# Two loads for x's first tiles and a new order of the opening in a dense Mish block

## The chip, the cores and the metric

The kernel runs on one NeuronCore of a Trainium2 chip. The metric is the device time of one execution in microseconds, as the median of several runs; lower is better. The profile comes from one execution taken by the hardware profiler, whose times are counted from the first instruction.

## The reference

```python
B, S, D, F = 1, 2048, 512, 1792     # all bf16
def reference(x, w1, b1, w2):
    h = jnp.einsum("bsd,df->bsf", x, w1) + b1
    sp = jnp.log1p(jnp.exp(-jnp.abs(h))) + jnp.where(h > 0, h, jnp.zeros_like(h))
    act = h * jnp.tanh(sp)          # Mish
    return jnp.einsum("bsf,fd->bsd", act, w2)
```

Two matrix products with a bias and the Mish activation between them: 2048 rows of 512 become 2048 rows of 1792, and then rows of 512 again.

## The kernel before

TensorE multiplies a stationary 128x128 tile with a moving tile of up to 512 columns, and contracts over the partitions. For the first product, x must therefore lie transposed, as `xT` (512 rows in KT = 4 tiles, named k, by 2048 columns); w1 lies as 4 tiles k by 1792 columns, in FT = 14 tiles named f. The 2048 rows of x are worked in four blocks of 512. For each block and each f, four matmuls (`mm1_step`, L176; one for each k) sum into one PSUM bank, ScalarE reads the bank with Mish and the bias (L159) into `a_sb`, and TensorE then makes the second product, 14 matmuls of 512 columns for each tile of 128 rows (`mm2_step`, L198). VectorE copies the result out of PSUM (L204), and SyncE stores it.

Every engine has a queue of its own which runs in the order in which the program writes it; the class `Stream` keeps for each a counter, and `wait` puts a semaphore wait into the queue. All order is thus written by hand.

The opening is special, since the data is still coming. TensorE runs eight matmuls on constants (`WARM`, L105) which serve no result. The first 256 rows of x are loaded as they lie into `x_nat`, one load for both tiles of 128, and TensorE transposes them by matmuls with an identity (`transpose_x`, L145): eight of 128 columns, in four PSUM banks, copied out into `xT` by VectorE and ScalarE (L150). Rows 256 to 511 and the other blocks come through transposing DMAs on SyncE's queue. Of w1, the first eight f (`OPEN`) are loaded as four pieces by k: k 0 and k 2 are issued by ScalarE, k 1 and k 3 by SyncE, all at L85. The first block's matmuls for these eight f then run k by k over eight PSUM banks, bank (4 + f) mod 8, in the order in which the pieces arrive (`first`): first k 0 for tile 0, and for tile 1, then k 1 and k 2 for both, then tiles 2 and 3 for k 0 to 2, and at the end k 3 for all 512 columns. `spread_b1` turns the bias on VectorE (L246, L248) before the first Mish needs it.

The two tiles of the first load hold even and odd rows of x, so that each partition reads one run of 2 KB; `rows` gives the stores of output tiles 0 and 1 the same order.

Of the kernel before, what the change touches and what calls it, by code (L numbers as in the profile page):

```python
# [4 lines left out]

P = 128
SQ = 32
WARM = (512,) * 5 + (256,) * 2 + (128,)
BLOCKS = (512, 512, 512, 512)


# [21 lines left out]
def bass_standalone__dense_activation_mish__prompt_kernel(  # L33
# [16 lines left out]
    x2, out2 = x[0], out[0]  # L50
# [3 lines left out]
    OPEN = 8  # L54
    N0 = BLOCKS[0] // P

    with ExitStack() as es:
        def sb(name, shape, t):
            return es.enter_context(nc.sbuf_tensor(name, shape, t))

        x_nat = sb("x_nat", [P, 2, D], BF)
        xT = sb("xT", [P, KT, S], BF)
# [5 lines left out]
        diff = sb("diff", [P, P], dt.int32)  # L68
        ident = sb("ident", [P, P], BF)
        a_sb = sb("a_sb", [P, FT, S], BF)  # L70
        o_sb = sb("o_sb", [P, S // P, D], BF)
        ps = es.enter_context(nc.psum_tensor("ps", [P, 8, 512], F32))

        def sem(name):
            return es.enter_context(nc.semaphore(name))

        sp = Stream(nc.sync, None)
        pe = Stream(nc.tensor, sem("c_pe"))
        dve = Stream(nc.vector, sem("c_dve"))
        act = Stream(nc.scalar, sem("c_act"))  # L80
        pool = Stream(nc.gpsimd, sem("c_pool"))

        def load(q, dst, src, name, transpose=False):
            s = sem(name)
            (q.eng.dma_start_transpose if transpose else q.eng.dma_start)(dst, src).then_inc(s, 16)  # L85
            return (s, 16)

        def load_w1(q, ks, a, b):
            return load(q, w1_sb[:, ks, a * P:b * P], w1v[:, ks, a * P:b * P], "s_w1_%d_%d" % (ks.start, a))
# [6 lines left out]
        def load_part(q, k0, k1, a, b):  # L96
            t = load_w1(q, slice(k0, k1), a, b)
            for f in range(a, b):
                for k in range(k0, k1):
                    t_w1[k, f] = t  # L100

        t_bz = dve.mark(nc.vector.memset(b1_nat[:, :], 0.0))  # L102
        c_w = nc.const_aps.tensor(1.0, [P, P], BF)
        c_m = nc.const_aps.tensor(1.0, [P, 512], BF)
        t_fill = [pe.mark(nc.tensor.matmul(ps[:, 7, 0:n], c_w, c_m[:, 0:n], start=True, stop=True)) for n in WARM]  # L105

        act.eng.preload_act_table(ACT.Mish)  # L107
        act.wait(t_bz)
        for k in (0, 2):
            load_part(act, k, k + 1, 0, OPEN)  # L110
        t_xn = load(sp, x_nat[:, :, :], x2[0:2 * P, :].rearrange("(p j) d -> p j d", p=P), "s_xn")
        load_part(sp, 1, 2, 0, OPEN)
        sp.wait(t_fill[2])
        t_x23 = load(sp, xT[:, :, 2 * P:4 * P], x2[2 * P:4 * P, :], "s_x23", True)
        load_part(sp, 3, 4, 0, OPEN)
# [3 lines left out]
        t = load(sp, w2_sb[:, :, :], w2v, "s_w2")  # L119
# [3 lines left out]
        for s in range(1, len(BLOCKS)):  # L123
            lo, hi = starts[s], starts[s + 1]
            t_xT.append(load(sp, xT[:, :, lo:hi], x2[lo:hi, :], "s_xT%d" % s, True))


        t_diff = pool.mark(pool.eng.iota(diff[:, :], pattern=[[1, P]], base=0, channel_multiplier=-1))  # L128
        dve.wait(t_diff)
        t_id = dve.mark(nc.vector.tensor_scalar(ident[:, :], diff[:, :], 0, None, ALU.is_equal))  # L130

        free = [[] for _ in range(8)]
        t_cp = {(j, k): t_x23 for j in (2, 3) for k in range(KT)}
        t_mish = {}

        def transpose_x():

            pe.wait(t_xn, t_id)
            for bank, (eng, js, ks) in enumerate(((dve, (0,), (0,)), (act, (1,), (0,)), (dve, (0, 1), (1,)),
                                                  (act, (0, 1), (2, 3)))):  # L140
                n, m = len(ks), len(js)
                for i, k in enumerate(ks):
                    for h, j in enumerate(js):
                        lo = (i * m + h) * P
                        mm = nc.tensor.matmul(ps[:, bank, lo:lo + P], x_nat[:, j, k * P:(k + 1) * P], ident[:, :],  # L145
                                              start=True, stop=True)
                eng.wait(pe.mark(mm))
                dst = xT[:, ks[0]:ks[0] + n, js[0] * P:(js[-1] + 1) * P]
                src = ps[:, bank, 0:n * m * P].rearrange("p (k t) -> p k t", k=n)
                t = eng.mark(nc.vector.tensor_copy(dst, src) if eng is dve else act.eng.activation(dst, src, ACT.Copy))  # L150
                for k in ks:
                    for j in js:
                        t_cp[j, k] = t
                free[bank] = [t]

        def mish(s, f, bank, t_mm):
            n = BLOCKS[s]
            act.wait(t_b1c, t_mm)
            t = act.mark(act.eng.activation(a_sb[:, f, starts[s]:starts[s + 1]], ps[:, bank, 0:n], ACT.Mish,  # L159
                                            bias=b1_sb[:, f:f + 1]))  # L160
            t_mish[s, f] = t
            free[bank] = [t]

        def mm1_step(s, f, k, bank, js=None):

            n = BLOCKS[s]
            lo, hi = (0, n) if js is None else (js[0] * P, (js[-1] + 1) * P)
            first = k == 0 and lo == 0
            if first:
                pe.wait(*free[bank])  # L170
            pe.wait(t_w1[k, f])
            if s:
                pe.wait(t_xT[s])
            else:
                pe.wait(*[t_cp[j, k] for j in (js or range(N0))])
            return nc.tensor.matmul(ps[:, bank, lo:hi], w1_sb[:, k, f * P:(f + 1) * P],  # L176
                                    xT[:, k, starts[s] + lo:starts[s] + hi], start=first, stop=(k == KT - 1 and hi == n))
# [8 lines left out]

        def rows(i):

            if i < 2:
                return out2[0:2 * P, :].rearrange("(p j) d -> p j d", p=P)[:, i, :]  # L190
            return out2[i * P:(i + 1) * P, :]

        def mm2_step(i, f, lo, hi, bank):
# [7 lines left out]
        def put(i, lo, hi, bank, t_mm, q=sp):  # L201
            nonlocal n_out
            dve.wait(t_mm)
            t = dve.mark(nc.vector.tensor_copy(o_sb[:, i, lo:hi], ps[:, bank, 0:hi - lo]))  # L204
            free[bank] = [t]
            q.wait(t)
            q.eng.dma_start(rows(i)[:, lo:hi], o_sb[:, i, lo:hi]).then_inc(s_out, 16)
            n_out += 1
# [8 lines left out]
        def mm2_last(i):  # L217

            nonlocal n_out
            cuts = (0, D - 3 * P // 2, D - P // 2, D)  # L220
            toks = []
            for n, eng in enumerate((dve, dve, act)):
                lo, hi, bank = cuts[n], cuts[n + 1], (i + n) % 4
                for f in range(FT):
                    mm = mm2_step(i, f, lo, hi, bank)
                eng.wait(pe.mark(mm))
                dst, src = o_sb[:, i, lo:hi], ps[:, bank, 0:hi - lo]
                t = eng.mark(nc.vector.tensor_copy(dst, src) if eng is dve else act.eng.activation(dst, src, ACT.Copy))  # L228
                toks.append((lo, hi, t))
            for q, lo, hi, t in ((sp, 0, toks[1][1], toks[1][2]), (act,) + toks[2]):  # L230
                q.wait(t)
                q.eng.dma_start(rows(i)[:, lo:hi], o_sb[:, i, lo:hi]).then_inc(s_out, 16)
                n_out += 1

        def first(fs, js, ks, last=False):
            for k in ks:
                for f in fs:
                    mm = mm1_step(0, f, k, (4 + f) % 8, js)
                    if last and k == KT - 1:
                        mish(0, f, (4 + f) % 8, pe.mark(mm))  # L240


        def spread_b1():
            dve.wait(t_b1)
            for j in range(P // SQ):
                t = dve.mark(nc.vector.transpose(b1_T[j * SQ:(j + 1) * SQ, :], b1_nat[:, j * SQ:(j + 1) * SQ]))  # L246
            dve.wait(t)
            return dve.mark(nc.vector.tensor_copy(b1_sb[:, :], b1_T[:, 0:FT]))  # L248

        transpose_x()  # L250
        t_b1c = spread_b1()
        first(range(4), (0,), (0,))
        first(range(4), (1,), (0,))
        first(range(4, OPEN), (0, 1), (0,))
        first(range(OPEN), (0, 1), (1, 2))
        first(range(OPEN), (2, 3), (0, 1, 2))
        first(range(OPEN), None, (3,), True)
# [42 lines left out]
```

## Time and profile before

| | |
|---|---|
| median of 3 runs | 104.91 us (104.37, 104.91, 105.55) |
| span of the profiled execution, first to last instruction | 104.0 us |
| TensorE busy | 101.4 us, 98% of the span, 520 matmuls |
| ScalarE busy | 39.5 us, 38% |
| VectorE busy | 13.2 us, 13% |
| bytes moved by DMA | 7.94 MB, mean 76 GB/s |

The profile gives for the profiled execution its span alone; what lies around the span, from the start of the execution to the first instruction and from the last to its end, is seen only in the runs' times, whose median lies 0.9 us above it. In the rows of the profile PE is a TensorE matmul, PEld its weight load, DVE VectorE, ACT ScalarE, POOL GpSimd and SP SyncE; SPq and ACTq are the issue of a DMA from that engine's queue. A row of the timeline has the start and the length in us of some instructions that follow each other, their number as x8, and in brackets how long the engine was idle before them and what ended the wait. A row by line and shape has after the bar the busy time in us, the mean of one instruction in ns, and the idle time before them. A row of a DMA gives its size and the us from issue to landing. A row for a stretch of time gives, after its ends, the busy time of all engines and of each with the number of instructions, then the granted clock, the DMA share and the GB/s.

### The profile page before, as it was taken

What the parts mean: (1) busy time and instruction counts of PE and PEld (TensorE: products, weight loads), DVE (VectorE), ACT (ScalarE), POOL (GpSimd) and SP (SyncE); (2) the same over time, 40 slices, a digit from 0 to 9 for tenths busy, and PEclk for the clock granted to TensorE, in tenths of its full rate; (3) what the DMA queues carried; (4) which work ended last, traced back from release to release, by engine and by line L of the source; (5) the groups of instructions that cost most, each with busy time, mean ns of one, the idle gap of its engine ahead of it and who ended that gap; (6) DMA issues with size and microseconds to landing.
All of it is one profiled execution on the core that took longest, in us unless ns stands there. A gap on an engine that the chain in (4) does not pass through costs nothing.

```text
span 104.0 us, 1180 instructions
## 1 busy us (share of the span) xinstructions
PE 101.4 (98%) x520; PEld 50.0 (48%) x520; DVE 13.2 (13%) x26; ACT 39.5 (38%) x60; POOL 0.4 (0%) x5
## 2 busy tenths in 40 slices
PE   7999999999999999999999999999999999999993
PEld 2888444444444444444444444444444444444472
DVE  1212000112220000022220000022112000021241
ACT  4300899300027777200007777500005777700000
POOL 1000000000000000000000000000000000000000
PEclk9999999999999999999999999999999999999999
DMA  2999999991101000010111000001111000001111
GB/s 70 367 295 368 359 223 193 199 204 50 50 3 47 0 0 6 0 50 12 39 50 50 0 0 3 0 6 50 50 50 50 0 0 0 0 0 56 52 50 50
DMA packets 12833, 7.94 MB, mean 76 GB/s; under 512 B 7836, under 2 KB 12188, under 8 KB 12828
## 3 DMA queue, kind: packets, MB, share of 16 engines
q1 hardware_dynamic: 12396, 7.33, 26.8%
q10 hardware_dynamic: 432, 0.54, 1.5%
q8 instruction: 4, 0.07, 0.3%
q14 instruction: 1, 0.01, 0.0%
HBM read 3.94 MB, written 2.10 MB: 58 GB/s over the span
## 4 chain that ended last, share of the span: by engine, by line
PE 98%; ACT 0%; issue 0%
PE ps L176 47%; PE ps L198 47%; PE ps L105 3%; PE ps L145 1%; ACT o_sb L228 0%
## 5 line engine op out<-in xcount | busy, mean ns | idle before, releaser
L159 ACT ACTIVATE a_sb<-ps,b_sb 128x512 bf16<-128x512 f32 x56 | 37.1, 698 | 48.5 <-PE ps L176 48.5
L176 PE MATMUL ps<-xT,w_sb 128*128 128x512 bf16 (+2 forms) x252 | 50.0, 361 | 0.0
L198 PE MATMUL ps<-w_sb,a_sb 128*128 128x512 bf16 (+3 forms) x252 | 49.1, 355 | 0.0
L176 PEld LDWEIGHTS ps<-xT,w_sb 128*128 128x128 bf16 x252 | 25.0, 101 | 24.1
L198 PEld LDWEIGHTS ps<-w_sb,a_sb 128*128 128x128 bf16 x252 | 23.2, 98 | 25.6
L204 DVE CAST o_sb<-ps 128x512 bf16<-128x512 f32 x15 | 10.4, 692 | 80.8 <-PE ps L198 80.8
L228 ACT ACTIVATE o_sb<-ps 128x64 bf16<-128x64 f32 x1 | 0.2, 224 | 11.5 <-PE ps L198 11.5
L105 PE MATMUL ps<-const-bfloat16-1.0 128*128 128x512 bf16 (+2 forms) x8 | 2.8, 532 | 0.8 <-PEq L285 0.8
L105 PEld LDWEIGHTS ps<-const-bfloat16-1.0 128*128 128x128 bf16 x8 | 1.0, 136 | 2.2 <-issue 2.1
L150 ACT ACTIVATE xT<-ps 128x128 bf16<-128x128 f32 (+1 forms) x2 | 0.9, 438 | 2.2 <-PE ps L145 2.2
L107 ACT ACT_TABLE_LOAD x1 | 1.3, 1283 | 0.7 <-PEq L285 0.7
L246 DVE STREAM_TRANSPOSE b_T<-b_nat 32x32 bf16<-32x32 bf16 x4 | 0.8, 202 | 3.1 <-DMA b_nat<-in_b_dram 3.0
L145 PE MATMUL ps<-ident,x_nat 128*128 128x128 bf16 x8 | 1.0, 309 | 0.0
L150 DVE CAST xT<-ps 128x128 bf16<-128x128 f32 (+1 forms) x2 | 0.7, 358 | 2.5 <-PE ps L145 2.4
L228 DVE CAST o_sb<-ps 128x320 bf16<-128x320 f32 (+1 forms) x2 | 0.8, 392 | 1.5 <-PE ps L198 1.5
L145 PEld LDWEIGHTS ps<-ident,x_nat 128*128 128x128 bf16 x8 | 0.8, 138 | 0.2 <-DMA x_nat<-in_x_dram 0.2
L130 DVE TENSOR_SCALAR ident<-diff 128x128 bf16<-128x128 int32 x1 | 0.2, 227 | 0.2 <-POOL diff L128 0.2
L128 POOL IOTA diff<- 128x128 int32 x1 | 0.2, 234 | 0.4 <-POOLq L285 0.4
L102 DVE MEMSET b_nat<- 32x64 uint32 x1 | 0.1, 112 | 0.8 <-PEq L285 0.8
L248 DVE CAST b_sb<-b_T 128x14 f32<-128x14 bf16 x1 | 0.2, 176 | 0.0
L285 POOL MEMSET const-bfloat16-1.0<- 128x1 bf16 x1 | 0.1, 101 | 0.0
L285 POOL MEMSET const-uint8-127<- 128x1 uint8 x1 | 0.1, 101 | 0.0
(2 smaller groups left out, 0.2 us busy)
## 6 DMA issues: line engine op xcount, KB each, us to landing
out_dram<-o_sb SPq DMA_DIRECT2D x15, 128.0 KB, 1.7
w_sb<-in_w_dram SPq DMA_DIRECT2D x1, 1792.0 KB, 10.5
w_sb<-in_w_dram SPq DMA_DIRECT2D x1, 768.0 KB, 5.8
w_sb<-in_w_dram ACTq DMA_DIRECT2D x2, 256.0 KB, 3.7
w_sb<-in_w_dram SPq DMA_DIRECT2D x2, 256.0 KB, 3.6
x_nat<-in_x_dram SPq DMA_DIRECT2D x1, 256.0 KB, 2.6
out_dram<-o_sb SPq DMA_DIRECT2D x1, 112.0 KB, 1.7
xT<-in_x_dram SPq DMA_TRANSPOSE x4, 5.2
```

What stands on the lines that cost most here:

```text
L105: t_fill = [pe.mark(nc.tensor.matmul(ps[:, 7, 0:n], c_w, c_m[:, 0:n], start=True, stop=True)) for n in WARM]
L107: act.eng.preload_act_table(ACT.Mish)
L128: t_diff = pool.mark(pool.eng.iota(diff[:, :], pattern=[[1, P]], base=0, channel_multiplier=-1))
L130: t_id = dve.mark(nc.vector.tensor_scalar(ident[:, :], diff[:, :], 0, None, ALU.is_equal))
L145: mm = nc.tensor.matmul(ps[:, bank, lo:lo + P], x_nat[:, j, k * P:(k + 1) * P], ident[:, :], start=True, stop=True)
L150: t = eng.mark(nc.vector.tensor_copy(dst, src) if eng is dve else act.eng.activation(dst, src, ACT.Copy))
L159: t = act.mark(act.eng.activation(a_sb[:, f, starts[s]:starts[s + 1]], ps[:, bank, 0:n], ACT.Mish, bias=b1_sb[:, f:f + 1]))
L176: return nc.tensor.matmul(ps[:, bank, lo:hi], w1_sb[:, k, f * P:(f + 1) * P], xT[:, k, starts[s] + lo:starts[s] + hi], start=first, stop=( ...
L198: return nc.tensor.matmul(ps[:, bank, 0:hi - lo], a_sb[:, f, i * P:(i + 1) * P], w2_sb[:, f, lo:hi], start=(f == 0), stop=(f == FT - 1))
L204: t = dve.mark(nc.vector.tensor_copy(o_sb[:, i, lo:hi], ps[:, bank, 0:hi - lo]))
L228: t = eng.mark(nc.vector.tensor_copy(dst, src) if eng is dve else act.eng.activation(dst, src, ACT.Copy))
L246: t = dve.mark(nc.vector.transpose(b1_T[j * SQ:(j + 1) * SQ, :], b1_nat[:, j * SQ:(j + 1) * SQ]))
```

## The change

The warm-up is shortened from 3200 columns to 2432, and a `BRIDGE` of 384 constant columns is put behind tile 0's transposes. x's first two tiles are loaded by two DMAs on SyncE's queue instead of one, each of 128 consecutive rows with 1 KB for each partition. Of w1's first eight f, k 0 stays the first load on ScalarE's queue; k 1 and k 2 become one load behind it, so that SyncE no longer issues k 1. `transpose_x` works on one tile: its k 0 goes to one bank and is copied by VectorE, its k 1 to 3 go to a second one and are copied by ScalarE. TensorE's order is now tile 0's transposes, the bridge, tile 0's k 0 for f 0 to 3, tile 1's transposes, tile 0's k 0 for f 4 and 5, tile 1's for f 0 to 5, and both tiles' for f 6 and 7; from k 1 on it is as before. Output tiles 0 and 1 are stored as the other tiles are. The iota of GpSimd is written at an earlier place in the program.

```diff
-WARM = (512,) * 5 + (256,) * 2 + (128,)
+WARM = (512,) * 4 + (256, 128)
+BRIDGE = (256, 128)
...
+        def load_tile(q, j):
+            return load(q, x_nat[:, j, :], x2[j * P:(j + 1) * P, :], "s_xn%d" % j)
+
         act.eng.preload_act_table(ACT.Mish)
         act.wait(t_bz)
-        for k in (0, 2):
-            load_part(act, k, k + 1, 0, OPEN)
-        t_xn = load(sp, x_nat[:, :, :], x2[0:2 * P, :].rearrange("(p j) d -> p j d", p=P), "s_xn")
-        load_part(sp, 1, 2, 0, OPEN)
+        t_xn = [load_tile(sp, 0), load_tile(sp, 1)]
+        load_part(act, 0, 1, 0, OPEN)
+        load_part(act, 1, 3, 0, OPEN)
+        t_diff = pool.mark(pool.eng.iota(diff[:, :], pattern=[[1, P]], base=0, channel_multiplier=-1))
         sp.wait(t_fill[2])
...
-        def transpose_x():
-
-            pe.wait(t_xn, t_id)
-            for bank, (eng, js, ks) in enumerate(((dve, (0,), (0,)), (act, (1,), (0,)), (dve, (0, 1), (1,)),
-                                                  (act, (0, 1), (2, 3)))):
-                n, m = len(ks), len(js)
+        def transpose_x(j):
+
+            pe.wait(t_xn[j], t_id)
+            for bank, ks, eng in ((2 * j, (0,), dve), (2 * j + 1, (1, 2, 3), act)):
+                n = len(ks)
                 for i, k in enumerate(ks):
-                    for h, j in enumerate(js):
-                        lo = (i * m + h) * P
-                        mm = nc.tensor.matmul(ps[:, bank, lo:lo + P], x_nat[:, j, k * P:(k + 1) * P], ident[:, :],
-                                              start=True, stop=True)
+                    mm = nc.tensor.matmul(ps[:, bank, i * P:(i + 1) * P], x_nat[:, j, k * P:(k + 1) * P], ident[:, :],
+                                          start=True, stop=True)
...
         def rows(i):
 
-            if i < 2:
-                return out2[0:2 * P, :].rearrange("(p j) d -> p j d", p=P)[:, i, :]
             return out2[i * P:(i + 1) * P, :]
...
-        transpose_x()
+        transpose_x(0)
+        for n in BRIDGE:
+            nc.tensor.matmul(ps[:, 7, 0:n], c_w, c_m[:, 0:n], start=True, stop=True)
+        first(range(4), (0,), (0,))
+        transpose_x(1)
         t_b1c = spread_b1()
-        first(range(4), (0,), (0,))
-        first(range(4), (1,), (0,))
-        first(range(4, OPEN), (0, 1), (0,))
+        first((4, 5), (0,), (0,))
+        first(range(6), (1,), (0,))
+        first((6, 7), (0, 1), (0,))
```

More of the change, by code (lines that the diff above doesn't have):

```diff
@@ L125, in bass_standalone__dense_activation_mish__prompt_kernel @@
             t_xT.append(load(sp, xT[:, :, lo:hi], x2[lo:hi, :], "s_xT%d" % s, True))
-        t_diff = pool.mark(pool.eng.iota(diff[:, :], pattern=[[1, P]], base=0, channel_multiplier=-1))
         dve.wait(t_diff)
@@ L134, in bass_standalone__dense_activation_mish__prompt_kernel @@
         t_mish = {}
-        def transpose_x():
-            pe.wait(t_xn, t_id)
-            for bank, (eng, js, ks) in enumerate(((dve, (0,), (0,)), (act, (1,), (0,)), (dve, (0, 1), (1,)),
-                                                  (act, (0, 1), (2, 3)))):
-                n, m = len(ks), len(js)
+        def transpose_x(j):
+            pe.wait(t_xn[j], t_id)
+            for bank, ks, eng in ((2 * j, (0,), dve), (2 * j + 1, (1, 2, 3), act)):
+                n = len(ks)
                 for i, k in enumerate(ks):
-                    for h, j in enumerate(js):
-                        lo = (i * m + h) * P
-                        mm = nc.tensor.matmul(ps[:, bank, lo:lo + P], x_nat[:, j, k * P:(k + 1) * P], ident[:, :],
-                                              start=True, stop=True)
+                    mm = nc.tensor.matmul(ps[:, bank, i * P:(i + 1) * P], x_nat[:, j, k * P:(k + 1) * P], ident[:, :],
+                                          start=True, stop=True)
                 eng.wait(pe.mark(mm))
-                dst = xT[:, ks[0]:ks[0] + n, js[0] * P:(js[-1] + 1) * P]
-                src = ps[:, bank, 0:n * m * P].rearrange("p (k t) -> p k t", k=n)
+                dst = xT[:, ks[0]:ks[0] + n, j * P:(j + 1) * P]
+                src = ps[:, bank, 0:n * P].rearrange("p (k t) -> p k t", k=n)
                 t = eng.mark(nc.vector.tensor_copy(dst, src) if eng is dve else act.eng.activation(dst, src, ACT.Copy))
                 for k in ks:
-                    for j in js:
-                        t_cp[j, k] = t
+                    t_cp[j, k] = t
                 free[bank] = [t]
```

## The prediction

> **What bounds the kernel now.** I read the chain that ended last first, then the list of waits, then the opening 10 us row by row, because the diff touches nothing behind them except the rows that two output stores write.
>
> ```profile
> span 104.0 us, 1180 instructions
> ...
> 13 pieces in order of time: start us, us, what
> 0.73 0.04 issue
> 0.77 2.82 PE ps L105 x8
> 3.60 0.85 PE ps L145 x8
> 4.45 13.01 PE ps L176 x84
> 17.46 12.09 PE ps L198 x56
> 29.55 12.09 PE ps L176 x56
> ...
> 102.18 0.22 ACT o_sb L228
> ```
>
> The chain is TensorE from 0.77 us to the end: warm-up (L105), eight transposes (L145), then matmuls without a hole. No data arrives late, so only two things can change the time: how many columns TensorE streams, and a hole that the new order opens. Two prices come from here. While the opening runs, eight transposes of 128 columns take 0.85 us: **0.107 us per 128 columns**. In the steady part 56 matmuls of 512 columns take 12.09 us: 0.216 each, **0.054 us per 128 columns**, half. The pace changes early:
>
> ```profile
> L176 PE MATMUL ps<-xT,w_sb 128*128 128x256 bf16 x4 | 1.1, 418 | 0.0
> ...
> L176 PE MATMUL ps<-xT,w_sb 128*128 128x256 bf16 x37 | 4.2, 272 | 0.0
> ...
> 5.95 0.57 PE L176 MATMUL ps<-xT,w_sb 128*128 128x256 bf16 x3
> ...
> 5.10:5.95 0.85, 0.85 (x6) 0.59 (x5) 1.00 1.26 301
> 7.00:7.85 0.85, 0.85 (x10) 0.76 (x8) 1.00 0.88 300
> ```
>
> The same 128x256 matmul takes 418 ns in 5.35 to 5.95 us and 272 ns in 6.60 to 10.30; two equal stretches hold 6 and 10 of them. The matmul that starts at 5.95 is the last slow one, so the switch is at about 6.1 us, 5.3 us after the first matmul. (The granted-clock column says 1.00 on both sides; the durations show the switch.) Below I call the paces slow and fast. If the switch stays where it is, a hole or a removed column **before** it is worth half its length at the end: what was not done slowly is done later at twice the pace.
>
> **What limits the opening.** The transposes follow the warm-up with a narrow margin over x:
>
> ```profile
> 3.07 0.53 PE L105 MATMUL ps<-const-bfloat16-1.0 128*128 128x256 bf16 x2
> 3.41 0.30 PE L145 MATMUL ps<-ident,x_nat 128*128 128x128 bf16 x1
> ...
> 3.40 0.14 PEld L145 LDWEIGHTS ps<-ident,x_nat 128*128 128x128 bf16 x2 [0.18 <-DMA x_nat<-in_x_dram]
> ...
> 0.74 0.40 SPq L85 DMA_DIRECT2D x_nat<-in_x_dram  x1
> ...
> 0.95 0.86 ACTq L85 DMA_DIRECT2D w_sb<-in_w_dram  x2
> ...
> 1.20 0.41 SPq L85 DMA_DIRECT2D w_sb<-in_w_dram  x1
> ...
> x_nat<-in_x_dram SPq DMA_DIRECT2D x1, 256.0 KB, 2.6
> ...
> w_sb<-in_w_dram ACTq DMA_DIRECT2D x1, 256.0 KB, 3.1
> ...
> w_sb<-in_w_dram SPq DMA_DIRECT2D x1, 256.0 KB, 3.6
> ...
> 2.00:4.00 2.00, 2.00 (x12) 1.19 (x11) 0.26 (x1) 0.18 (x2) 0.00 (x0) 1.00 0.93 331
> ```
>
> Issue plus time to landing: x at 0.74 + 2.6 = 3.34 us, w1's k 0 at 0.95 + 3.1 = 4.05, k 1 at 1.20 + 3.6 = 4.80. They land in turn, SyncE's ring, ScalarE's, SyncE's, at 331 GB/s and a DMA share of 0.93: the engines are full, so what moves earlier is what has fewer bytes ahead of it. The warm-up ends where the first transpose starts, 3.41 us: it was as long as x's way here, and k 0 landed 0.2 us ahead of its first use at 4.25 (3.41 + 8 x 0.107).
>
> **The change, part by part.**
>
> *Warm-up and bridge.* 512 + 256 = 768 columns leave the warm-up, 6 x 0.107 = 0.64 us: it ends at 3.41 - 0.64 = 2.77. The bridge puts back 384 columns, 0.32 us. Net 0.32 us less filler at the slow pace. All useful columns stay: the same eight transposes, and the k 0 step has 8 x 128 + 4 x 256 columns before, 12 x 128 + 2 x 256 after. Two 128-column matmuls instead of one of 256 cost nothing at the slow pace, where a pitch of 0.107 holds with a weight load each; at the fast pace I have no such pair and bound it by the weight load:
>
> ```profile
> L176 PEld LDWEIGHTS ps<-xT,w_sb x3: 98/98/98, 7.7 to 7.9; 128*128 128x128 bf16 x3
> ```
>
> That is 2 x 0.098 for 2 x 0.054, so up to four pieces x 0.044, 0.18 us, if the switch came before them; with the switch at 6.1 they lie ahead of it, and I take 0.
>
> *Tile 0's load.* It has 128 KB instead of 256: 131 KB at 331 GB/s is 0.40 us, so it lands at 3.34 - 0.40 = 2.94. The ends: 3.34 if the fixed part of the 2.6 us rules and bytes don't, 2.77 or earlier if the half load is quicker than in proportion. x now comes in 1 KB pieces instead of 2 KB; w2 comes in 1 KB pieces as well, and where it streams alone the rate is no lower:
>
> ```profile
> 10.00:12.00 2.00, 2.00 (x14) 1.13 (x12) 0.00 (x0) 1.12 (x2) 0.00 (x0) 1.00 1.09 368
> ```
>
> So I add nothing for the pieces. TensorE, done with filler at 2.77, waits for 2.94 plus the 0.06 from landing to weight load (3.34 to 3.40 in the rows): **hole 1, 0.23 us**, between 0 and 0.63.
>
> [...]
>
> *Tile 0's first copy and k 0.* The transposes start at 3.00 and end at 3.43, the bridge ends at 3.75. The copy: before, from first transpose to copy and the copy itself:
>
> ```profile
> 3.74 0.74 DVE L150 CAST xT<-ps 128x128 bf16<-128x128 f32 x2 [2.42 <-PE ps L145]
> ...
> L150 DVE CAST xT<-ps 128x128 bf16<-128x128 f32 x1 | 0.3, 292 | 2.4 <-PE ps L145 2.4
> L150 ACT ACTIVATE xT<-ps 128x512 bf16<-128x512 f32 x1 | 0.6, 597 | 0.4 <-PE ps L145 0.4
> L150 ACT ACTIVATE xT<-ps 128x128 bf16<-128x128 f32 x1 | 0.3, 278 | 1.8 <-PE ps L145 1.8
> ```
>
> 3.74 - 3.41 = 0.33, plus 0.29, plus about 0.05 for the signal: ready 0.67 after the first transpose, at 3.67, inside the bridge. Without the bridge it would be a hole of 0.24. k 0, second in turn, has 131 KB less ahead of it: 4.05 - 0.40 = 3.65, also inside. If tile 1 went ahead of it in the engines, k 0 would stay at 4.05 and open 0.3 us. I take no hole; the four matmuls end at 3.75 + 0.43 = 4.18.
>
> *Tile 1.* The new wait for its load stands in TensorE's queue with all later matmuls behind it. Its issue takes the place that k 1's had at 1.20 in SyncE's queue, and it is third in turn with 131 KB of its own instead of 262: 4.80 - 0.80 = 4.00, before 4.18. The bound is 4.4 if the ScalarE ring's second load gets ahead of it. Its transposes end at 4.61, the two matmuls of f 4 and 5 at 4.82. The copy of its k 0 is ready 0.67 after the first transpose, at 4.85: **hole 2, 0.05 us** with the restart. Then six matmuls to 5.51. Those of f 6 and 7 need bank 3 back from ScalarE's copy of 384 elements: 0.49 us between the 278 and 597 rows, started 0.25 behind the last transpose's end at 4.61, so done by 5.35. They end at 5.94.
>
> *The rest.* The k 1 step thus begins at 5.94, against 5.95 before. k 1 and 2 as one load have the same bytes ahead of their end as k 2 before, landing by 5.7; k 1 gets later than its old 4.80 but needed only at 5.94. On SyncE the wait for the third warm-up matmul and the x transposes behind it stay where they were, since the third matmul does. The bias spreading stays behind the copies on VectorE and waits for its own load far later:
>
> ```profile
> 7.48 0.90 DVE L246 STREAM_TRANSPOSE b_T<-b_nat 32x32 bf16<-32x32 bf16 x4 [3.00 <-DMA b_nat<-in_b_dram]
> ...
> 10.88 7.63 ACT L159 ACTIVATE a_sb<-ps,b_sb 128x512 bf16<-128x512 f32 x13 [5.79 <-PE ps L176]
> ```
>
> It is done by 8.6, the first activation comes at 10.88: 2.2 us of cover. GpSimd's iota is only written earlier; its queue holds nothing else. The first two output stores change rows, not bytes.
>
> **The sum.** Filler -0.32, hole 1 +0.23, hole 2 +0.05: -0.04 us before the switch, -0.02 at the end. The profiled span of 104.0 becomes 104.0. The median of the runs, 104.9, lies 0.9 above that span (launch edges and another execution), and I carry this over: **104.9 us, no change**. Ends of the terms: no holes gives -0.32/2 = -0.16 at the end; hole 1 of 0.63 gives +0.2.
>
> **Rivals.**
>
> *Tile 0 lands by 2.8*, no hole 1: the first pieces of x wait on memory, not on bytes, and a lone tile could beat proportion. Then 104.75, and if the filler were worth its whole 0.32, 104.6. Against it: x left the engines at full share.
>
> *The change doesn't do what it says*: tile 0 lands at 3.34 as the pair did, or k 0 stands behind tile 1. The holes grow to 0.6 to 0.9, at half worth, less 0.16: 105.05 to 105.2.
>
> *The switch comes late.* That is the slow side. TensorE has had no hole from 0.77 to 6.1. If the fast pace needs an unbroken run as long as this one, 5.3 us, the last hole, at 4.85, restarts it and the switch comes at 10.2: 4.1 us more at the slow pace lose 2.05 us, 107.0 in all. It decides from the first hole that the hardware counts as idle. For it: the switch was late enough that something before 6.1 had to be complete. Against: the holes are 0.28 of some 5 us, so TensorE is over 90% busy. [...] No row here decides the one or the other.
>
> **How the numbers follow.** The forecast has 0.50, no hole 0.17, more holes 0.20, the late switch 0.10, others 0.03. The three runs of the kernel before already lie 1.18 us apart (104.37 to 105.55), so a new median can move by some 0.5 us by itself; 1%, 1.05 us, is about what a measurement can tell from no change. The range runs from 104.2 (no hole, a quick set of runs) to 105.8 (more holes, a slow set, or a switch only partly late). Faster by over 1% needs 103.9, which no case reaches without luck: 0.06. Slower: the late switch and the tail of more holes, 0.14.
>
> **What would show it.** Right: first transpose near 3.0 with a DMA wait of about 0.2 before it, tile 0 landing 2.2 us after its issue, no gap before L176's first matmul, k 1's step near 5.9, the pace switching at one point. Wrong: a switch after 8 us (late-switch rival); no wait ahead of the transposes; a gap of 0.3 or more at k 0 or at tile 1; any new hole behind 6 us.

## The result

| | median | runs | ratio to the kernel before |
|---|---|---|---|
| before | 104.95 us | 6, 104.37 to 105.55 | |
| changed | 106.06 us | 6, 105.23 to 107.93 | 1.0101, 95% interval 1.0055 to 1.0147 |

The change makes the kernel slower by about 1%, 1.1 us at the medians; no change had been forecast. The ratios, here and below, leave out runs over 1.5% above the fastest of the same kernel (107.93 here; 106.78 and 107.02 of the hole alone; 106.57 of the join alone; 107.73, 107.79 and 108.08 of k 2 on the other queue; 154.46 in the square), and the medians in us keep them. Each run now also comes with the span of its own execution: the changed kernel's profiled execution took 105.23 us for a span of 103.9, so **1.3 us lie around the span**, not 0.9. By that count the profiled execution of before (span 104.0) took about 105.3 us, in the slow half of its kernel, and the one of the changed kernel is the fastest of its six. The two profiles that one would lay side by side are a slow execution of the faster kernel and a fast one of the slower.

The page of the changed kernel, and its chain that ended last, in order of time (start, length, what):

```profile
span 103.9 us, 1175 instructions
...
PE 95%; DMA 2%; issue 1%; ACT 0%
```

```profile
0.67 0.07 issue
0.74 2.40 DMA x_nat<-in_x_dram
3.14 0.05 issue
3.18 0.61 PE ps L145 x4
3.79 0.32 PE ps L249 x2
4.11 0.43 PE ps L175 x4
4.54 0.43 PE ps L145 x4
4.97 5.52 PE ps L175 x50
```

The chain no longer starts with the warm-up but with x's load: tile 0 lands at 3.14 us and TensorE has waited. The timeline has this wait in brackets, and one ahead of the k 1 step:

```profile
3.18 0.13 PEld L145 LDWEIGHTS ps<-ident,x_nat 128*128 128x128 bf16 x2 [0.59 <-DMA x_nat<-in_x_dram]
3.18 0.29 PE L145 MATMUL ps<-ident,x_nat 128*128 128x128 bf16 x1 [0.23 <-DMA x_nat<-in_x_dram]
...
5.94 0.11 PEld L175 LDWEIGHTS ps<-xT,w_sb 128*128 128x128 bf16 x2 [0.18 <-DMA w_sb<-in_w_dram]
```

The second is new: the k 1 step starts at 5.94 as computed, but only because the load that holds k 1 and k 2 has just landed. Its row, size and us from issue (it is issued at 1.36, so 5.9):

```profile
w_sb<-in_w_dram ACTq DMA_DIRECT2D x1, 512.0 KB, 4.5
```

In this execution the weight load waits 0.2 us there, and the matmuls run on without a hole (the chain has one piece from 4.97 to 10.49). A second profile of the same kernel, below, shows another execution.

### The profile page after: what moved, and what is told of

It reads as the page before. It is cut to its first block, busy times and chain, and to the rows that moved or that the text cites. A ratio compares the mean times of both kernels' runs of the same rounds, so it can differ in the third digit from the quotient of the medians.

```text
span 103.9 us, 1175 instructions
## 1 busy us (share of the span) xinstructions
PE 100.6 (97%) x513; PEld 49.7 (48%) x522; DVE 13.1 (13%) x26; ACT 39.5 (38%) x60; POOL 0.4 (0%) x5
## 4 chain that ended last, share of the span: by engine, by line
PE 95%; DMA 2%; issue 1%; ACT 0%
PE ps L175 47%; PE ps L195 46%; DMA x_nat<-in_x_dram 2%; PE ps L145 1%; PE ps L249 0%; ACT o_sb L225 0%
## 5 line engine op out<-in xcount | busy, mean ns | idle before, releaser
L175 PE MATMUL ps<-xT,w_sb 128*128 128x512 bf16 (+2 forms) x249 | 49.5, 358 | 0.3
L106 PE MATMUL ps<-const-bfloat16-1.0 128*128 128x512 bf16 (+2 forms) x6 | 2.2, 537 | 0.8 <-PEq L286 0.8
L150 ACT ACTIVATE xT<-ps 128x384 bf16<-128x384 f32 x2 | 1.0, 490 | 2.5 <-DVE xT L150 1.8
L150 DVE CAST xT<-ps 128x128 bf16<-128x128 f32 x2 | 0.6, 292 | 3.1 <-PE ps L145 3.1
L249 PE MATMUL ps<-const-bfloat16-1.0 128*128 128x256 bf16 (+1 forms) x2 | 0.5, 368 | 0.0
```

## The experiments

All ratios are to the kernel before on the same chip. Theory 1 was that holes near 3 us make the fast pace late.

**The hole filled.**

```diff
-WARM = (512,) * 4 + (256, 128)
+WARM = (512,) * 5 + (256,) * 2 + (128,)
```

> The changed kernel with the old warm-up of 3200 columns in place of 2432 (and the bridge kept), so that TensorE has no hole ahead of tile 0's transposes. Theory 1, the holes make the fast pace come later: without hole 1 the switch is back where it was, and the only loss against the kernel before is 384 columns more of filler at the slow pace, 0.32/2 = 0.16, so 105.0 to 105.3 us, faster than the changed kernel by 0.8 to 1.0. Rival, tile 0 simply lands later in most executions than in the profiled one and the switch does not move: a hole filled with filler is as long as an empty one, so about 106.0 as the changed kernel.

Measured: 106.1 us, 1.0109 (1.0074 to 1.0143). Nothing is won back. Hole 1, the wait for tile 0, is not where the changed kernel's 1% is; if it costs anything there, the filler put in its place, or something behind it, takes the gain away. The profiled execution was the fastest of the nine, 105.06 us: there the joined load landed 4.3 us from its issue, no piece of it took over 0.23 us, and TensorE did not wait for w1. What the others waited for was not traced in this kernel.

**The hole alone.** The kernel before with

```diff
-WARM = (512,) * 5 + (256,) * 2 + (128,)
+WARM = (512,) * 4 + (256, 128)
```

> The kernel before with the short warm-up of 2432 columns and nothing else changed: one load of x, the old order. The warm-up then ends at 2.75 us and x lands at 3.36, a hole of 0.65 in place of 0.64 of filler. Theory 1 (a hole makes the switch late): at least as slow as the changed kernel, 106 to 107 us. Rival (the switch stays, or the loss comes from the two loads or the new order): 104.9 to 105.0, no change against the kernel before.

Measured: 105.58 us, 1.0033 (0.9998 to 1.0068). Two of its twelve runs took 106.78 and 107.02 us; no run of the kernel before, in any of these comparisons, is above 105.72. The timeline shows the hole, x having come too late for the first transpose:

```profile
2.00 0.95 PE L105 MATMUL ps<-const-bfloat16-1.0 128*128 128x512 bf16 x3
3.44 1.03 PE L145 MATMUL ps<-ident,x_nat 128*128 128x128 bf16 x8 [0.48 <-DMA x_nat<-in_x_dram]
```

From the warm-up's last column, 2.75 us, to 3.44 that is 0.69 us in place of 0.64 of filler. A fixed switch would make it free (0.03), theory 1 wanted 1 us or more. It cost about 0.35, with an interval from 0 to 0.7: that speaks against theory 1, but can't tell 0.35 from free by itself. The bench below gives a reason for a value between the two.

**The changed kernel again.**

> The changed kernel once more, for a second profile and more runs: 105.7 to 106.4 us. If this profile is a slower one than the first (span 103.9), theory 1 expects the same landings and a pace that switches later than the first profile's 5.7 us, by 2 us for each us of span; the rival expects tile 0 to land later than 3.14 by the difference in span and a switch near 5.7.

Measured: 105.9 us, 1.0102 (1.0068 to 1.0135), so the result repeats. Neither theory had this profile, of an execution of 106.19 us. First the timeline, then the stretch of the wait (its length of 1.35 us, of which TensorE was busy 0.25; at the end of the row the DMA share and the GB/s):

```profile
6.90 0.33 PEld L175 LDWEIGHTS ps<-xT,w_sb 128*128 128x128 bf16 x4 [1.34 <-DMA w_sb<-in_w_dram]
6.90 0.50 PE L175 MATMUL ps<-xT,w_sb 128*128 128x256 bf16 x3 [1.16 <-DMA w_sb<-in_w_dram]
```

```profile
5.50:6.85 1.35, 0.25 (x2) 0.06 (x1) 0.00 (x0) 0.00 (x0) 0.00 (x0) 1.00 0.72 129
```

TensorE has finished k 0 at 5.6 and stands for more than a microsecond, with the DMA engines at a share of 0.72 and 129 GB/s. It waits for the joined load, 5.5 us from its issue at 1.36:

```profile
w_sb<-in_w_dram ACTq DMA_DIRECT2D x1, 512.0 KB, 5.5
x_nat<-in_x_dram SPq DMA_DIRECT2D x2, 128.0 KB, 2.5
```

And it got there early, because in this execution the pace had switched before 5.1 us. The same 128-column matmuls in 5.12 to 5.40 us, here and then in the first profile of the changed kernel:

```profile
L175 PE MATMUL ps<-xT,w_sb 128*128 128x128 bf16 x6 | 0.5, 221 | 0.0
```

```profile
L175 PE MATMUL ps<-xT,w_sb 128*128 128x128 bf16 x5 | 0.8, 309 | 0.0
```

A hole that is ended by a landing swallows whatever is saved ahead of it, which may be why the filled hole won nothing. Theory 2: k 1 carries the token of 512 KB (the one semaphore that says that the whole joined load has landed), and that comes too late.

**When the pace switches, by itself.** 60 bursts of matmuls on constants, each after TensorE had stood idle for some 12 us:

> Computes nothing of the reference (it stores zeros): 60 bursts of matmuls on constants, each after 14 us or more of idle TensorE. A burst has 2.0 us of warm-up as the changed kernel's, then no wait, or a wait for a chain of four VectorE copies that ends before the warm-up (control), or 0.2, 0.45, 0.7 or 1.0 us after it, then 48 small matmuls. Measured is the time from a burst's first matmul to the fast pace. Theory 1: the time grows with the hole, by more than the hole's own length for 0.45 us and over, about 1 to 3 us. Rival: the same mean time, 3.4 to 5.5 us, for all six kinds.

The chains were shorter than planned: the kinds meant as 0.2, 0.45, 0.7 and 1.0 gave idle times of 0, 0.18, 0.43 and 0.73 us. These are counted from a matmul's last column, 0.107 us after its start for 128 columns; the busy time in the rows below ends with the modelled end of the matmul, 0.2 us later. Here the trace records the granted clock. Columns: stretch, us, busy us of TensorE, weight loads, VectorE and GpSimd, then the clock. A burst without a hole, two with 0.43, and two with 0.73:

```profile
510.52:513.60 3.08, 3.08 (x14) 1.73 (x15) 0.00 (x0) 0.00 (x0) 0.50 0.00 0
513.60:515.60 2.00, 2.00 (x19) 1.78 (x18) 0.00 (x0) 0.00 (x0) 1.00 0.00 0
```

```profile
1097.57:1100.69 3.12, 2.89 (x12) 1.37 (x13) 1.73 (x4) 0.00 (x0) 0.50 0.00 0
1100.69:1102.69 2.00, 2.00 (x20) 1.77 (x19) 0.00 (x0) 0.00 (x0) 1.00 0.00 0
1223.98:1226.99 3.01, 2.78 (x11) 1.29 (x12) 1.73 (x4) 0.00 (x0) 0.50 0.00 0
1226.99:1230.40 3.41, 3.41 (x18) 2.42 (x16) 0.00 (x0) 0.00 (x0) 0.50 0.02 5
1230.40:1232.40 2.00, 2.00 (x20) 1.76 (x18) 0.00 (x0) 0.00 (x0) 1.00 0.00 0
```

```profile
489.74:493.12 3.38, 2.85 (x12) 1.32 (x13) 2.03 (x4) 0.00 (x0) 0.50 0.00 0
493.12:495.12 2.00, 2.00 (x19) 1.78 (x18) 0.00 (x0) 0.00 (x0) 1.00 0.00 0
612.73:616.00 3.27, 2.74 (x11) 1.27 (x12) 2.03 (x4) 0.00 (x0) 0.50 0.00 0
616.00:619.41 3.41, 3.41 (x18) 2.41 (x17) 0.00 (x0) 0.00 (x0) 0.50 0.00 0
```

In this trace all 60 switches, over 1.2 ms, lay on one grid of 3.413 us that did not follow the bursts' starts (their times modulo 3.4133 agree within 0.01; those of the five bursts above, 493.12 to 1230.40, are 6, 31, 141 and 38 steps apart). The burst that reached a grid point after 3.12 us with 0.43 idle got the fast pace there; the one that reached it after 3.01 did not, and got it 3.41 later. With 0.73 idle the limit lay between 3.27 and 3.38. I read both as one rule, an estimate from these bursts: the pace came at the first grid point that had **2.58 to 2.65 us of TensorE work** between it and the burst's first matmul (3.01 - 0.43 was too little, 3.38 - 0.73 enough). The bursts do not show over how long a stretch that work is counted, nor what a hole of over 0.73 us does. Neither theory was right. The holes restarted nothing, since the bursts with 0.43 and 0.73 us had the pace 3.12 and 3.38 us after their first matmul; and the switch did not stay either. By this estimate a hole of h, up to the 0.73 us of the bursts, delays the earliest grid point that counts by h, and if the grid is at random against the kernel, the switch by h on average. No run shows that it is; the profiles have the switch before 5.1, near 5.7 and at 6.1 us.

So by this estimate a hole before the switch costs half its length as lost work and half as a later switch, **its whole length on average**, while filler taken away saves half. For the hole alone that is 0.69 - 0.64/2 = 0.37, and 0.35 was measured, with the wide interval above. By the two paces an execution that just misses a grid point pays 3.41/2 = 1.7 us. That alone does not explain the two high runs of the hole alone: they lie 2.3 and 2.6 us above its lowest, 104.46.

**The join undone.** In the changed kernel

```diff
-        load_part(act, 1, 3, 0, OPEN)
+        load_part(act, 1, 2, 0, OPEN)
+        load_part(act, 2, 3, 0, OPEN)
```

> The changed kernel with w1's k 1 and k 2 as two loads on ScalarE's queue instead of one; all else as changed. Theory 2 (formed from the second profile of the changed kernel, where TensorE waits 1.3 us for the joined load, landing at 6.86 us): what costs the 1% is that k 1 carries the token of a load of 512 KB, which ends beside the x transposes. Then k 1 lands by 5.0 us, no hole ahead of its step, and the time is 105.0 to 105.3 us (the kernel before plus at most 0.4 for the earlier holes). Theory 1 (the holes near 3 us and the late switch): no change against the changed kernel, 105.8 to 106.2.

Measured: 105.47 us, 1.0053 (1.0020 to 1.0086). Half of the loss goes, though the interval overlaps that of the changed kernel (1.0068 to 1.0135). k 1 landed 3.6 us from its issue. Its list of waits (total, times, longest) has 0.3 us for w1, where the second profile of the changed kernel has 1.7; it lies at k 0:

```profile
PEld ps L146 <- DMA x_nat<-in_x_dram: 0.4, 1, 0.4
PEld ps L176 <- DMA w_sb<-in_w_dram: 0.3, 1, 0.3
```

**The join alone.** The kernel before with ScalarE's loads as in the changed one, and k 1 gone from SyncE:

```diff
-        for k in (0, 2):
-            load_part(act, k, k + 1, 0, OPEN)
+        load_part(act, 0, 1, 0, OPEN)
+        load_part(act, 1, 3, 0, OPEN)
...
-        load_part(sp, 1, 2, 0, OPEN)
```

> The kernel before with k 1 and k 2 as one load behind k 0 on ScalarE's queue, and k 1 taken from SyncE's; one load of x, the old warm-up and the old order. Theory 2: 105.6 to 106.3 us, the changed kernel's loss almost whole, with a hole of 0.3 to 1.5 us ahead of the k 1 step. Theory 1, or the two loads of x being the cause: 104.9, no change against the kernel before.

Measured: 105.18 us, 1.0037 (1.0002 to 1.0072). A third of the loss, where theory 2 wanted nearly all: with one load of x the joined load landed 4.3 us from issue, near 5.7, and its profile has no wait for w1. In that execution the pace was still slow at 6.4 us, so it can't show what an early switch does.

**k 2 on the other queue.** In the changed kernel

```diff
-        load_part(act, 1, 3, 0, OPEN)
+        load_part(act, 1, 2, 0, OPEN)
+        load_part(sp, 2, 3, 0, OPEN)
```

> The changed kernel with k 1 alone as ScalarE's second load, and k 2 on SyncE's queue behind the two tiles of x. Theory 2: as the split on one queue, 105.0 to 105.3 us; k 1 lands by 5.0, k 2 by 5.7. Theory 1: 105.8 to 106.2.

Measured: 106.15 us, 1.0083 (1.0043 to 1.0124), a miss for theory 2. k 1 is a load of its own here, second on ScalarE's queue, and still lands 5.6 us from its issue:

```profile
w_sb<-in_w_dram ACTq DMA_DIRECT2D x1, 256.0 KB, 5.6
```

So the join isn't the only thing that makes k 1 late. The packets show it, the pieces in which the DMA engines move a load: two of its 2 KB pieces, begun at 3.80 us, took 0.84 and 1.35 us; the usual one takes 0.08. Single w1 pieces of 0.5 to 0.9 us, begun at 3.4 to 4.2 us, are in the traces of the changed kernel and the split as well, while in that of before no 2 KB piece took over 0.31 us (there 1.5 KB pieces of the rest of w1, begun at 6.7 to 7.2 us, took up to 0.80). That made theory 3: the two loads of x bring them about.

**The x transposes later.** In the changed kernel

```diff
-        sp.wait(t_fill[2])
+        sp.wait(t_fill[5])
```

> The changed kernel with SyncE's x transposes (and all loads behind them) waiting for the last warm-up matmul instead of the third, 0.7 us later. It tells why the joined load lands late. If the transposes, which begin at 4.6 to 4.8 us, slow its last pieces: it lands by 5.6 in all executions, the hole ahead of k 1 shrinks to 0.4 or less, and the time is 105.2 to 105.7 us unless tiles 2 and 3, now landing near 7.3, open a hole of their own. If the load's own 512 KB are the whole reason, it lands as before and the time stays 105.8 to 106.2 or more.

Measured: 105.62 us, 1.0052 (1.0019 to 1.0085), as much of a gain as the split's and as uncertain. The edit did less than it was meant to: the issue of the x transposes moved from 2.24 to 2.99 us, but their first piece still moved at 4.8, as in the changed kernel (4.8 and 4.9). The trace speaks against the transposes as the cause: the joined load took 5.4 us all the same, and the pieces of it that stalled, for 0.7 to 1.0 us, were begun at 3.6 to 3.9, before a transpose piece had moved. TensorE came to the k 1 step at the slow pace (314 ns for 128 columns up to 5.8 us) and waited nevertheless:

```profile
w_sb<-in_w_dram ACTq DMA_DIRECT2D x1, 512.0 KB, 5.4
...
6.80 0.39 PE L175 MATMUL ps<-xT,w_sb 128*128 128x256 bf16 x2 [0.70 <-DMA w_sb<-in_w_dram]
```

**The loads by themselves.**

> Computes nothing of the reference (it stores zeros): the opening's loads by themselves, 12 rounds of six patterns, each begun when all of the last have landed: the loads as before, as changed, as changed with k 1 and 2 split, as before with k 1 and 2 joined, as changed with tiles 2 and 3 by a plain load instead of the x transposes, and as changed with k 2 on SyncE's queue. Read is when the load that k 1 needs has landed, from the first x issue. Theory 2 (the join makes k 1 late): as before 4.0 to 4.4 us; joined, and changed, 5.0 and later with a spread of up to 1.5; split and k 2 on SyncE as before. Theory 3 (formed from the profiles of the last four: single pieces of w1 stall by 0.5 to 1.3 us behind tile 1's, so the two loads of x make k 1 late by themselves): split and k 2 on SyncE are late and spread in many rounds too, joined with one load of x is not. If the x transposes are what the join collides with, the plain pattern is early and narrow.

When the load that holds k 1 has landed, us from the first x issue, in 12 rounds of each pattern, and how many w1 pieces on ScalarE's queue took over 0.4 us:

```
pattern                               min  median   max   slow pieces
old: one x, k 1 on SyncE              4.25   4.37   4.46        2
joined: one x, k 1 and 2 joined       4.78   4.88   5.02        2
changed: two x, k 1 and 2 joined      4.85   4.93   6.02       13
plain: as changed, no x transposes    4.67   4.94   6.42       17
split: two x, k 1, k 2 apart          4.02   4.22   4.80       39
k 2 on SyncE: two x, k 1, k 2 apart   3.95   4.11   4.60        5
```

Neither theory is right alone. Theory 2 had the joined load late and spread with one load of x too; theory 3 had k 1 late also where the loads are apart. What the bench has is the two **together**. Joining cost 0.5 us (4.88 against 4.37), with hardly any spread as long as x was one load (4.78 to 5.02). Two loads of x added slow pieces, 13 to 39 against 2 (5 in the last pattern, where 14 pieces of k 2 on SyncE's queue are slow as well). Only where both met did k 1 have a late tail: 5.6 to 6.0 in four of twelve rounds of the changed pattern, up to 6.4 without any transposes. Slow pieces as such are not peculiar to two loads: in the joined pattern 65 of x's own 2 KB pieces took over 0.4 us, all begun within 1.4 us of the issue. One round each, first old, then changed:

```profile
w_sb<-in_w_dram ACTq DMA_DIRECT2D x2, 256.0 KB, 4.0
w_sb<-in_w_dram SPq DMA_DIRECT2D x2, 256.0 KB, 3.9
x_nat<-in_x_dram SPq DMA_DIRECT2D x1, 256.0 KB, 3.2
xT<-in_x_dram SPq DMA_TRANSPOSE x1, 4.5
...
w_sb<-in_w_dram ACTq DMA_DIRECT2D x1, 512.0 KB, 5.2
x_nat<-in_x_dram SPq DMA_DIRECT2D x2, 128.0 KB, 2.9
w_sb<-in_w_dram ACTq DMA_DIRECT2D x1, 256.0 KB, 3.1
w_sb<-in_w_dram SPq DMA_DIRECT2D x1, 256.0 KB, 4.6
xT<-in_x_dram SPq DMA_TRANSPOSE x1, 5.2
```

Where a piece stalled, the 256-byte pieces of the transposes stood too, up to 0.8 us in the first changed round and 1.3 in the second profile of the changed kernel, and all ended together, 0.2 us after the last piece of the joined load in the second profile. It looks as if they wait for the engine that is behind, which is argued; k 3's first piece moved 1.0 us later there than in the first profile (7.1 against 6.1). With k 2 on SyncE the bench has k 1 early in all twelve rounds; it does not reproduce the 5.6 us of the kernel above.

**A square.** TensorE's order, the warm-up of 3200 columns and the bridge are the same in four kernels; they differ in the loads (and, with one load of x, in the rows of the first two output stores). Where k 1 and k 2 are apart, k 1 is on SyncE's queue with one load of x and on ScalarE's with two. The first of the four is the filled hole, above. Old loads:

```diff
-        t_xn = [load_tile(sp, 0), load_tile(sp, 1)]
-        load_part(act, 0, 1, 0, OPEN)
-        load_part(act, 1, 3, 0, OPEN)
+        for k in (0, 2):
+            load_part(act, k, k + 1, 0, OPEN)
+        t_xn = [load(sp, x_nat[:, :, :], x2[0:2 * P, :].rearrange("(p j) d -> p j d", p=P), "s_xn")] * 2
+        load_part(sp, 1, 2, 0, OPEN)
```

> The new order of TensorE with the old loads: the loads as in the kernel before (one for both tiles of x, k 1 on SyncE), the warm-up of 3200 columns, and the changed kernel's bridge, transposes and k 0 order. It differs from the run with the filled hole in the loads alone. If the loads are the cause (theories 2 and 3): the kernel before plus the bridge's 0.16, so 104.9 to 105.2 us. If the new order costs something by itself: 105.6 or more.

Two loads of x, and the join undone (the filled hole with the diff of the split):

> The changed kernel with the warm-up of 3200 columns and k 1 and k 2 as two loads: neither hole 1 nor the join, only the two loads of x, k 1 on ScalarE's queue, and the new order are left. Theory 2 with the late switch as the rest: 104.9 to 105.2 us. Theory 3 (the two loads of x delay single pieces of w1): 105.4 to 105.8, no better than the split with hole 1.

One load of x, and the join (the old loads with the diff of the join alone):

> The fourth corner of a square in which TensorE's order, the warm-up of 3200 columns and the bridge are the same: k 1 and 2 joined, x as one load. The others are at 1.0022 (apart, one load of x), 1.0031 (apart, two loads) and 1.0109 (joined, two loads) of the kernel before. If the join alone is to blame, 1.009 to 1.011, 105.7 to 105.9 us. If the join costs only what its own 512 KB cost and the two loads of x make the rest (the bench of the loads: joined lands 4.78 to 5.02 behind x's issue with one load of x, 4.85 to 6.02 with two), 1.003 to 1.006, 105.0 to 105.4 us, with a hole of 0.5 us or less ahead of the k 1 step.

| | one load of x | two loads of x |
|---|---|---|
| k 1 and k 2 apart | 1.0022 (0.9990 to 1.0054), 105.14 us | 1.0031 (0.9991 to 1.0070), 105.17 us |
| k 1 and k 2 joined | 1.0041 (1.0010 to 1.0072), 105.31 us | 1.0109 (1.0074 to 1.0143), 106.10 us |

Theory 3 alone had the upper right at 105.4 to 105.8 us, theory 2 alone the lower left at 105.7 to 105.9; both missed. The three other corners lie within 0.2% of each other, where the bridge's 0.16 us (0.15%) would put them, or a little above. Only the corner with both is at 1%, and its interval is clear of the others', though only just (1.0074 against 1.0072). The new order costs nothing that can be measured.

## Why the prediction was wrong

*Which step failed.* "k 1 gets later than its old 4.80 but needed only at 5.94", with the joined load "landing by 5.7". Both halves failed, and I had costed the edit at nothing on them. The load landed at 5.9 and 6.9 in the two profiles: "the same bytes ahead of their end" counts bytes at a steady rate, which gives the middle (the bench's median of 4.93, with x's issue at 0.74, is 5.7) and leaves out single pieces that stall (0.5 to 1.35 us in the profiles). And 5.94 was worked out with the slow pace to 6.1 us, where one execution had its switch. By the estimate from the bench the switch comes some 2.6 to 6 us after the first matmul (2.6 of work, and up to 3.41 to the next grid point); with one before 5.1, as in the second profile, TensorE is at k 1 at 5.6. The cover that I named was whole only in executions with a late switch, and the profile of before was of one; with stalled pieces not even a late switch was enough, as the run with the later transposes shows (0.70 us of waiting).

*What it measured.* The join's own cost with two loads of x is 0.8 us in the square (1.0109 - 1.0031), and 0.5 where hole 1 is kept (1.0102 - 1.0053); each is the difference of two ratios with intervals of about 0.35 us to either side, so it is good to about 0.5 us.

*The half price.* "A hole or a removed column before it is worth half its length at the end" holds, by the estimate from the bench, for the column and not for the hole. Hole 1 was 0.43 us in the first profile (0.23 forecast, between its ends of 0 and 0.63), hole 2 0.06 (0.05 forecast): at whole price less 0.16 for the filler that is +0.3 and not -0.02. (In the second profile it was 0.15, 0.23 at k 0 and 0.06: the same sum.) By these prices filling hole 1 costs 0.32 and saves 0.15 to 0.43, so the filled hole had little to win. The short warm-up alone measured about this price, 0.35, with an interval from 0 to 0.7.

*The late switch.* The rival had the right engine and the wrong rule: no unbroken run of 5.3 us is asked for, since the burst above without a hole had the pace after 3.08. That a switch misses a grid point can be in the scatter of every kernel here, the one before included (104.3 to 105.7 us). Something near its 107.0 is not ruled out, though: seven of the 63 runs of kernels with the short warm-up took 106.8 to 108.1 us, and none of the 160 others, the one of 154.46 aside. None of the seven was traced.

*More holes.* This rival came closest: it had the opening's landings stay late, for 105.05 to 105.2. It looked at k 0 and tile 1, which were nearly in time (0.04 us of hole and none in the first profile, 0.23 and none in the second), and priced holes at half.

*What held.* Warm-up's end (2.75), first transpose (3.18 and 2.90 against 3.00), the first copy under the bridge, the 0.05 from a copy's end to the matmul behind it (5.15 to 5.20 in the chain of the filled hole), tile 1's landing ahead of its use, hole 2 and 1 KB pieces at little loss (46 ns at the median against 84 for 2 KB). *The carry from span to time* was off by 0.4 us, which a forecast of no change does not feel.

*Left open.* Why single w1 pieces stall for 0.5 to 1.3 us when x comes as two loads, and why k 1 as ScalarE's second load was late in the kernel with k 2 on SyncE, which is slower by 0.8% without any join, but never in the bench. What delays the seven runs above 106.7 us: two of them, 107.93 and 108.08, have a mean granted clock of 0.984, which over a span of 106.6 us is 3.4 us at half, one step of the grid. That the rest of the split's loss, 0.53%, is hole 1 and hole 2 alone (0.3 by their price) is argued and within its interval, not shown.

## What to carry to other kernels

The token of the joined load covered all 512 KB, and came 4.5 and 5.5 us from its issue in the two profiles: before two loads are joined, ask when the first consumer needs the first half, in the fastest execution and not in the one that was profiled. One profile shows one place of the switch (before 5.1, near 5.7 and at 6.1 us in three of them here); cover that comes from a slow stretch is cover only while that stretch lasts, and the spans of several runs tell on which side the profiled one lay. By the estimate from the bench a hole in TensorE ahead of the switch costs its length and filler only half of its own (0.35 us measured for 0.69 of hole in place of 0.64 of filler, 0.37 by the estimate, interval 0 to 0.7), so filler that reaches to the first landing would be the cheaper of the two.

## What the runs showed of the hardware

In the bench of the switch TensorE's fast pace came on a grid of 3.413 us (60 switches), at the first grid point with 2.58 to 2.65 us of TensorE work since the burst's first matmul (an estimate; the bounds are from the bursts with 0.43 and 0.73 us of hole). In the bench of the loads, with x's 256 KB as one load, w1's pieces on ScalarE's queue took over 0.4 us 4 times in 24 rounds; as two loads of 128 KB, 74 times in 48. In the square the two loads of x and the join each cost at most 0.4% by themselves (1.0031 and 1.0041) and both together 1.1% (1.0109).
